# Bucketed attention and a two-layer network on one core: most first-batch heads loaded into both partition halves, operands made by factors per partition, score scale in the queries

## The chip, the cores and the metric

The kernel runs on one core of one Trainium2 chip. The metric is the device time of one execution in microseconds. Engines are named as in the profile: PE does matmuls and PEld loads their weights, DVE, ACT and POOL are the three elementwise engines, SP issues the DMAs. Three runs of the kernel before took 937.56, 939.98 and 940.53 us; the median, 939.98 us, is the time before.

## What is computed

Attention with a mask by hash buckets, and behind it a two-layer network with an exact gelu on the concatenated heads:

```python
batch, n_heads, seq, head_dim = (4, 8, 768, 64)      # q, k, v
q_bits = (np.einsum('bhsd,dk->bhsk', q, proj) > 0)   # proj: 64 x 6
k_bits = (np.einsum('bhsd,dk->bhsk', k, proj) > 0)
mask = q_bucket[:, :, :, None] == k_bucket[:, :, None, :]     # all six bits equal
scores = scale * np.matmul(q, k.transpose(0, 1, 3, 2))        # scale = 1 / sqrt(64)
scores = np.where(mask, scores, -1000000000.0)
attn = np.exp(scores - np.max(scores, axis=-1, keepdims=True))
attn = attn / (np.sum(attn, axis=-1, keepdims=True) + 1e-09)
out = np.matmul(attn, v)
...
h = x @ w_in                    # x: 3072 tokens x 512, w_in: 512 x 2048
g = 0.5 * h * (1.0 + erf(h * inv_sqrt2))
return (g @ w_out)              # w_out: 2048 x 512
```

## The kernel before

**Passes.** The four batches are walked in order. The first batch is done in two passes: pass 0 takes query columns 0 to 255 of all eight heads, pass 1 columns 256 to 767 of the eight heads in reverse order. The last three heads of pass 0 are made for all 768 queries and their operands are kept for pass 1 (`KEEP = 3`), so the first batch has 8 + 5 = 13 head loads. Batches 1 to 3 are one pass of eight heads each, 24 loads. A unit is 128 queries of one head against all 768 keys; there are 192, and 48 of them are in the first batch.

**A head** (`head`). Queries and keys of a head lie in one 128 x 768 tile: the queries transposed in partitions 0 to 63 (called the upper half here), the keys in 64 to 127 (the lower half). One DMA (L618) loads it into `rawe` (pass 0) or `raw` (later), rings of one buffer each. Then `high` (L621) rounds the tile to the fast matmul format into `Aq`. Three copies (`add_move`) put the rounded queries into the upper half of `Bq`, the rounded keys into the lower half of `Bk` and the rounded keys into the upper half of `Ak`; each may be on ACT, DVE, POOL (L377, L380) or a DMA (L625). Two subtractions raw minus rounded (`add_low`, L400, on DVE or POOL) give the low parts: of the queries into `Bq`'s lower half, of the keys into `Bk`'s upper half. Where operand sets share storage with the tiles of the later stage, the profile calls them `x` and `rest`.

**The hash.** Projections of both halves (L673, L675, L678) go to PSUM, their signs to `sign` (L681), and `mask_q` and `mask_k` write the signs as twelve extra rows into the lower halves of `Aq` and `Ak`, so that the score matmul adds a huge negative number for every bit that differs. The rest of those halves is zero (the clears at L338 and L434), or meets zeros.

**A unit** (`unit`). Scores come from two accumulating matmuls for each half of the keys (L716 on `Aq`, `Ak`; L717 on `Bq`, `Bk`). DVE takes the row maximum, negated (L720). `guard` (L724) makes the factor SCALE, or 0 where a row has no key in its bucket, and `shift` (L729) multiplies the maximum by it; both work on one column. ACT does the exp with this factor and shift (L732). In pass 0 and for three head pairs of pass 1 the whole probabilities are transposed by matmuls with a diagonal (L789), evicted to `pt` by ACT or DVE (L377, L380) and multiplied with the values in the slow format (L837). Elsewhere they are split in two halves (L748), transposed by DMA and multiplied by L846.

**The network.** Weights arrive as 64-bit words, are decoded on DVE (L466, L471, L476), scaled and split into high and low halves (`weight_pair`). The hidden layer is L1025, the gelu L1059, the output layer L1093.

**The order.** Nothing of the order is found at run time. `Plan.order` walks a model of the engines: each step has a key (a due time, from the numbers in `PAR`), a cost for each engine it may use, and the steps and buffers that it needs; the free engine takes the ready step with the lowest key. The steps of the network have late keys and are put wherever PE would be free. A step that may use several engines is placed by the first of them that is free and by the biases in `PAR` (such as `EV_ACT`). Each engine then executes its list in that order. DMAs all go through SP's list.

## Time and profile before

| | |
|---|---|
| median of three runs | 939.98 us |
| profiled execution, its own time | 939.12 us |
| its span | 937.3 us |
| mean granted PE clock | 0.987 |
| busy: PE, DVE, ACT, POOL | 883.2, 728.6, 612.7, 303.4 us |
| DMA | 122.81 MB in 300806 packets |

The span is the time from the first to the last instruction that the profiler recorded; the execution's own time is 1.8 us longer. Busy time is a share of the whole span, while the kernel has stages, so it is read by stretches of time. A matmul's record reaches into that of the next one, so mean durations of PE rows are longer than their distance.

### The profile page before, as it was taken

The page shows a single profiled execution, that of the slowest core. Times are in us where ns is not written, and L with a number is a line of the kernel's source. Part 1 is how long each engine was busy: PE and PEld are TensorE (multiplying, and loading weights), DVE is VectorE, ACT ScalarE, POOL GpSimd, SP SyncE. Part 2 cuts the span into 40 slices and gives each one's busy share as a digit, 9 for nine tenths or more (in the row PEclk, how much of TensorE's full clock was granted, in tenths as well). Part 3 has the DMA queues.
Part 4 walks back from the last instruction along what each step waited for, and adds up shares of the span by engine and source line. Part 5 has one row for each costly group of instructions (what it writes and reads, how often), then busy time and mean ns, then how long its engine had stood idle before and what let it go on. Part 6 is the DMA issues. An engine that isn't in the chain of part 4 may idle for free.

```text
span 937.3 us, 17819 instructions
## 1 busy us (share of the span) xinstructions
PE 883.2 (94%) x6728; PEld 642.8 (69%) x6728; DVE 728.6 (78%) x1616; ACT 612.7 (65%) x976; POOL 303.4 (32%) x254
## 2 busy tenths in 40 slices
PE   4777999887999999999999999999999999999998
PEld 3565788766676766677767776766777767676763
DVE  7899989899989899988889999989889971212122
ACT  5776877879776885867876777776788652222221
POOL 3652654556432233533142432342533100000000
PEclk9789999999999999999999999999999999999999
DMA  9456255277878699886787988687885850000000
GB/s 266 124 169 211 71 143 154 65 180 143 168 132 172 136 196 181 177 142 149 144 173 146 204 152 194 129 166 164 156 154 110 150 102 24 4 20 24 1 23 23
DMA packets 300806, 122.81 MB, mean 131 GB/s; under 512 B 241328, under 2 KB 285488, under 8 KB 300720
## 3 DMA queue, kind: packets, MB, share of 16 engines
q1 hardware_dynamic: 300544, 121.67, 59.5%
q8 instruction: 53, 0.87, 0.4%
q14 instruction: 33, 0.27, 0.1%
q10 hardware_dynamic: 176, 0.00, 0.0%
HBM read 45.49 MB, written 6.29 MB: 55 GB/s over the span
## 4 chain that ended last, share of the span: by engine, by line
PE 59%; DVE 7%; DMA 4%; ACT 3%; issue 1%; POOL 0%; ACTq 0%; SPq 0%; POOLq 0%; DVEq 0%
PE hp L1093 21%; PE hp L1025 21%; PE hp L846 6%; PE s L716 5%; PE s L717 4%; DVE hl L748 2%; DVE rows L720 2%; DMA vraw<-v 1%; DMA pt<-wraw 1%; DMA pt<-hl 1%; ACT p L732 1%; PE hp L673 1%; DVE wraw L748 1%; PE hp L678 1%; PE hp L675 1%
## 5 line engine op out<-in xcount | busy, mean ns | idle before, releaser
L1025 PE MATMUL hp<-x,Win 128*128 128x256 f16 x2304 | 267.9, 273 | 1.2 <-DVE rows L724 1.2
L1093 PE MATMUL hp<-Wout,g 128*128 128x512 f16 x1152 | 261.6, 379 | 0.0
L1025 PEld LDWEIGHTS <-Win 128*128 128x128 f16 x2304 | 220.3, 98 | 42.2 <-issue 13.5
L1093 PEld LDWEIGHTS <-g 128*128 128x128 f16 x1152 | 108.6, 98 | 128.4 <-issue 9.2
L720 DVE TENSOR_REDUCE rows<-s 128x1 f32<-128x768 f32 x192 | 179.5, 950 | 13.9 <-PE s L717 13.0
L732 ACT ACTIVATE p<-s,rows 128x768 f32<-128x768 f32 x143 | 141.3, 988 | 40.5 <-DVE rows L729 26.5
L716 PE MATMUL s<-Ak,Aq 128*128 128x384 f32 x352 | 137.8, 391 | 12.3 <-ACT p L732 6.0
L1035 ACT ACTIVATE h<-hp,ffs 128x512 f32<-128x512 f32 x96 | 65.8, 685 | 120.9 <-PE hp L1025 118.1
L717 PE MATMUL s<-Bk,Bq 128*128 128x384 f32 x352 | 120.5, 342 | 0.0
L380 DVE TENSOR_SCALAR g<-h,ffs 128x512 f16<-128x512 f32 x39 | 20.4, 526 | 112.4 <-ACT h L1059 81.7
L716 PEld LDWEIGHTS s<-Ak,Aq 128*128 128x128 f32 x352 | 67.6, 192 | 35.5 <-ACT p L732 12.4
L846 PE MATMUL hp<-pt,vhl 128*64 128x256 f16 x1368 | 82.3, 274 | 0.8 <-DMA pt<-hl 0.8
L846 PEld LDWEIGHTS <-vhl 128*64 128x64 f16 x1368 | 71.7, 110 | 12.7 <-issue 12.2
L1073 DVE SCALAR_TENSOR_TENSOR g<-h,ffs,g 128x512 f16<-128x512 f32 x96 | 77.0, 821 | 2.4
L748 DVE SCALAR_TENSOR_TENSOR hl<-p,rows,hl 128x768 f16<-128x768 f32 x72 | 76.2, 1061 | 2.1 <-ACT hl L377 1.0
L789 PE MATMUL hp<-dr,p 128*128 128x128 f32 x480 | 65.0, 290 | 6.3 <-DVE pt L380 2.4
L789 PEld LDWEIGHTS hp<-dr,p 128*128 128x128 f32 x480 | 61.1, 202 | 12.9 <-issue 3.3
L717 PEld LDWEIGHTS s<-Bk,Bq 128*128 128x128 f32 x352 | 68.0, 193 | 1.1
L732 ACT ACTIVATE wraw<-s,rows 128x768 f32<-128x768 f32 x49 | 48.4, 988 | 15.3 <-DVE hl L748 5.9
L681 ACT ACTIVATE sign<-hp,off 44x256 f32<-44x256 f32 (+1 forms) x74 | 41.6, 572 | 23.0 <-PE hp L678 21.0
L400 POOL TENSOR_TENSOR Bq<-raw,Aq 64x768 fp32r<-64x768 f32 (+1 forms) x23 | 40.9, 1779 | 22.6 <-ACT Aq L377 12.9
L380 POOL TENSOR_SCALAR hl<-p,rows 128x768 f16<-128x768 f32 x24 | 26.6, 1109 | 60.5 <-DMA pt<-hl 49.9
(154 smaller groups left out, 1258.9 us busy)
## 6 DMA issues: line engine op xcount, KB each, us to landing
raw<-qk SPq DMA_DIRECT2D x29, 384.0 KB, 3.6
vraw<-v SPq DMA_DIRECT2D x25, 384.0 KB, 4.1
wraw<-w_in SPq DMA_DIRECT2D x16, 512.0 KB, 4.3
wraw<-w_out SPq DMA_DIRECT2D x16, 512.0 KB, 5.1
out<-o SPq DMA_DIRECT2D x12, 512.0 KB, 2.8
Ak<-Aq SPq DMA_DIRECT2D x19, 192.0 KB, 3.3
rawe<-qk SPq DMA_DIRECT2D x8, 384.0 KB, 3.3
Bk<-Aq SPq DMA_DIRECT2D x16, 192.0 KB, 3.2
```

The source lines that it names most:

```text
L380: on.tensor_scalar(out=out, in0=in_, scalar1=scale, scalar2=bias, op0=ALU.mult, op1=ALU.add)
L716: nc.tensor.matmul(to, aq[:, qs], ak[:, n], start=True, stop=False)
L717: nc.tensor.matmul(to, bq[:, qs.start - q0 : qs.stop - q0], bk[:, n], start=False, stop=True)
L720: nc.vector.tensor_reduce(out=nm, in_=both(sp), axis=AX.XY, op=ALU.max, negate=True)
L732: nc.scalar.activation(out=buf(ex).rearrange("p (b k) -> p b k", b=2), in_=both(sp), func=AF.Exp, scale=sc, bias=nb, accum_out=ssum,)
L748: nc.vector.scalar_tensor_tensor(out=buf(hi)[:, 1], in0=buf(ex), scalar=r, in1=buf(hi)[:, 0], op0=ALU.mult, op1=ALU.subtract,)
L789: nc.tensor.matmul(buf(step[0])[:, (k - k0) * P : (k - k0 + 1) * P], buf(ex)[:, words(k)], buf(dg), start=True, stop=True,)
L846: nc.tensor.matmul(pv[j * D : (j + 1) * D], buf(vh)[:, tv, kt, j * D : (j + 1) * D], buf(holds[j][0])[:, tp * KT + kt, :nt], start=kt == 0 ...
L1025: nc.tensor.matmul(buf(pair[0])[:, j * ch[1] : (j + 1) * ch[1]], win_hl[:, f0 // WB1, tw, pr, f0 % WB1 : f0 % WB1 + P], x[:, tx, pr, : ch[1]],
L1035: nc.scalar.activation(out=bufs["h"][0][:, 2 * fp : 2 * fp + 2, :nt], in_=buf(pair[0])[:, : 2 * nt].rearrange("p (j k) -> p j k", j=2), fu ...
L1073: nc.vector.scalar_tensor_tensor(out=gt[:, 1, s2, :nt], in0=h[:, s2, :nt], scalar=sg, in1=gt[:, 0, s2, :nt], op0=ALU.mult, op1=ALU.subtract,)
L1093: nc.tensor.matmul(buf(banks[u]).rearrange("p (c f) -> p c f", c=NWB), gt[:, tg, f, u * P : (u + 1) * P], wout_hl[:, :, tw, ft], start=ft ...
```

## The change

`head` gets an argument `twice`, true for the first batch except for the first two heads of pass 0 (`OLD = 2`): eleven head loads. For these:

- The keys are loaded twice, into both halves of a raw buffer, and the queries twice, into both halves of another one; only the columns that are needed. These are four DMAs in place of one. `raw` and `rawe` get two buffers each.
- No copies are made. A factor per partition does the work of the halves: `Ak` is the loaded keys times (1, 0), rounded; `Bk` is the loaded keys times (-1, 1) plus `Ak`, so minus the low part above and the keys themselves below; `Aq` is the queries times SCALE, rounded; `Bq` is the queries times (0, SCALE) minus `Aq`. The two roundings may be on ACT, DVE or POOL, the two others are `scalar_tensor_tensor` on DVE.
- The projection takes one matmul more for each stretch of columns in which queries are projected, since high queries and high keys are in separate tiles; its constants are `hash_lo`, `hash_neg` and `hash_both`.
- The early operand sets hold only 256 queries in `Aq` too, and `Ak` is cleared for the first two sets only.

For the 26 other heads the rounding has a factor per partition (SCALE for queries, 1 for keys), and the low part of the queries is a `scalar_tensor_tensor` on DVE only. For all units the score scale is thus in the queries, and `guard` and `shift` become one instruction over two columns. `sign` is bf16. All numbers of `PAR` are others, and it has four new ones (`QL`, `QH0` to `QH2`).

```diff
-RAWE = 1
+RAWE = 2
+RAWS = 2
+OLD = 2
...
-        "s": 2, "hp": 4, "p": 2, "hl": 2, "raw": 1, "rawe": RAWE, "sign": 1, "dr": 2, "pt": NTH + 1,
+        "s": 2, "hp": 4, "p": 2, "hl": 2, "raw": RAWS, "rawe": RAWE, "sign": 1, "dr": 2, "pt": NTH + 1,
...
-        "sign": ring(const, "sign", [2 * 32, S], F32, 1),
+        "sign": ring(const, "sign", [2 * 32, S], BF16, 1),
...
-            early.tile([P, q_first if nm == "Bq" else S], F32R, tag=f"{nm}{i}", name=f"{nm}{i}")
+            early.tile([P, q_first if nm[1] == "q" else S], F32R, tag=f"{nm}{i}", name=f"{nm}{i}")
...
+    nc.gpsimd.memset(rows[:, :, 0], 1.0)
+    only_up, only_low, minus_up, fold = factors = [
+        const.tile([P, 1], F32, tag=f"half{i}", name=f"half{i}") for i in range(4)
+    ]
+    for t, (up, down) in zip(factors, ((1.0, 0.0), (0.0, SCALE), (-1.0, 1.0), (SCALE, 1.0))):
+        nc.gpsimd.memset(t[:D], up)
+        nc.gpsimd.memset(t[D:], down)
...
+    nc.vector.tensor_scalar(
+        out=hash_neg[:, both_bits], in0=hash_hi[:, both_bits].bitcast(F32), scalar1=minus_up, scalar2=None,
+        op0=ALU.mult,
+    )
...
-    for n, (_, ak, _, _) in enumerate(sets[1:]):
+    for n, (_, ak, _, _) in enumerate(sets[:OLD]):
...
+        if twice:
+            def add_load(half, cols, more):
+                box = []
+                def load():
+                    n = cols.stop - cols.start
+                    for to in range(2):
+                        nc.sync.dma_start(
+                            out=buf(box[0])[to * D : (to + 1) * D, :n], in_=qk[b, h, half * D : (half + 1) * D, cols]
+                        )
+                n = cols.stop - cols.start
+                box.append(
+                    add("SP", 0.02 + 1.84e-3 * n, load, key - PAR["HQ"] + more, takes="rawe" if first else "raw")
+                )
+                return box[0]
+            rk = add_load(1, slice(0, S), 0)
+            rq = add_load(0, qr, PAR["QL"])
+            def key_high():
+                affine(hk.engine, ak, buf(rk), only_up)
+            def key_low():
+                nc.vector.scalar_tensor_tensor(
+                    out=bk, in0=buf(rk), scalar=minus_up, in1=ak.bitcast(F32), op0=ALU.mult, op1=ALU.add
+                )
+            def query_high():
+                affine(hq.engine, aq[:, qb], buf(rq)[:, :nq], SCALE)
+            def query_low():
+                nc.vector.scalar_tensor_tensor(
+                    out=bq[:, qb], in0=buf(rq)[:, :nq], scalar=only_low, in1=aq[:, qb].bitcast(F32),
+                    op0=ALU.mult, op1=ALU.subtract,
+                )
+            hk = add(affine_on("RND", S, True), 0, key_high, key, [rk, *clear], port=True)
+            lk = add("DVE", subtract_cost("DVE", S), key_low, key + PAR[f"LOW{cl}"], [hk], port=True)
+            hq = add(affine_on("RND", nq), 0, query_high, key + PAR[f"QH{cl}"], [rq, *clear], port=True)
+            lq = add("DVE", subtract_cost("DVE", nq), query_low, key + PAR[f"DUP{cl}"], [hq], port=True)
+            free(rk, [lk])
+            free(rq, [lq])
...
-            affine(hi.engine, aq, buf(raw))
+                affine(hi.engine, aq, buf(raw), fold)
...
-        lq = add_low(nq, bq[D:, qb], top, qr)
+            def query_low():
+                nc.vector.scalar_tensor_tensor(
+                    out=bq[D:, qb], in0=buf(raw)[:D, qr], scalar=SCALE, in1=aq[:D, qr].bitcast(F32),
+                    op0=ALU.mult, op1=ALU.subtract,
+                )
...
-                nc.tensor.matmul(pp, hash_lo, aq[:, n], start=True, stop=False)
+                if twice and with_q:
+                    nc.tensor.matmul(pp, hash_lo[:, KR:], aq[:, at], start=True, stop=False)
+                if twice:
+                    nc.tensor.matmul(pp, hash_lo[:, :HR], ak[:, n], start=not with_q, stop=False)
+                else:
+                    nc.tensor.matmul(pp, hash_both, aq[:, n], start=True, stop=False)
...
-            nc.vector.tensor_scalar(
-                out=sc, in0=nm, scalar1=BIG / 2, scalar2=SCALE, op0=ALU.is_lt, op1=ALU.mult
-            )
-        def shift():
-            nc.vector.tensor_scalar(out=nb, in0=nm, scalar1=sc, scalar2=None, op0=ALU.mult)
+            nc.vector.scalar_tensor_tensor(
+                out=st[:, 2:4], in0=nm.broadcast_to([P, 2]), scalar=BIG / 2, in1=st[:, :2],
+                op0=ALU.is_lt, op1=ALU.mult,
+            )
...
+                twice = b == 0 and (n_pass > 0 or pos >= OLD)
```

More of the change, by code (lines that the diff above doesn't have):

```diff
@@ L280, in tile_bucket_attention_moe @@
     ]
[L281 removed]
+    rows = const.tile([P, NT, 7], F32, tag="rows", name="rows")
     tiny = const.tile([P, 4 * NSC + 2 * B, 4], F32, tag="tiny", name="tiny")
@@ L606, in values_halves, with head @@
         return hi, lo
-    def head(b, h, i, key, clear, qr, cl):
+    def head(b, h, i, key, clear, qr, cl, twice):
         aq, ak, bq, bk = sets[i]
@@ L640, in add_low @@
-        def add_low(n, out, rows, cols):
-            box = []
-            box.append(
-                add(
-                    subtract_on("LO", n), 0,
-                    lambda: subtract(box[0].engine, out, buf(raw)[rows, cols], aq[rows, cols].bitcast(F32)),
-                    key + PAR[f"LOW{cl}"], [hi], port=True,
-                )
-            )
-            return box[0]
-        top, end = slice(0, D), slice(D, P)
-        raw = add("SP", 1.43, load, key - PAR["HQ"], takes="rawe" if first else "raw")
@@ L665, in head @@
+        space = add("none", 0, lambda: None, key, [lq, lk], takes="sign")
         signs = []
@@ L684, in sign @@
                 )
-            box.append(add("PE", 0.04 + (0.46e-3 * (2 + with_q)) * (c1 - c0), project, key + PAR[f"PRJ{cl}"], [space], takes="hp"))
+            box.append(add("PE", 0.04 + (0.46e-3 * (2 + (1 + twice) * with_q)) * (c1 - c0), project, key + PAR[f"PRJ{cl}"], [space], takes="hp"))
             signs.append(add("ACT", affine_cost("ACT", c1 - c0, True) + 0.09, sign, key + PAR[f"PRJ{cl}"], box))
@@ L695, in mask_k, with unit @@
             affine(r2.engine, ak[D : D + 2 * NBIT], rows, BIG / 2, -BIG / 2)
-        r1 = add(affine_on("MSK", nq), 0, mask_q, key + PAR[f"MSK{cl}"], [*signs, m2, m3], port=True)
+        r1 = add(affine_on("MSK", nq), 0, mask_q, key + PAR[f"MSK{cl}"], [*signs, *masked], port=True)
         r2 = add(affine_on("MSK", S), 0, mask_k, key + PAR[f"MSK{cl}"], signs, port=True)
         free(space, [r1, r2])
-        return [m3, r1, r2]
-    def unit(t, i, q0, qs, cl, whole, made, place):
+        return [*masked[1:], r1, r2]
+    def unit(t, i, q0, qa, qs, cl, whole, made, place):
         aq, ak, bq, bk = sets[i]
         st = rows[:, t % NT]
-        nm, sc, nb, ssum, si, r = (st[:, k : k + 1] for k in range(6))
+        nm, sc, nb, ssum, si, r = (st[:, k : k + 1] for k in range(1, 7))
         def both(step):
@@ L763, in unit @@
         mx = add("DVE", 0.87, top, t - PAR[f"MX{cl}"], [sp])
-        sh = add("DVE", 0.07, guard, t - PAR[f"EX{cl}"], [mx])
-        sh = add("DVE", 0.07, shift, t - PAR[f"EX{cl}"], [sh])
+        sh = add("DVE", 0.1, guard, t - PAR[f"EX{cl}"], [mx])
         ex = add("ACT", 0.98 + 0.23 * (si_on == "ACT"), exps, t - PAR[f"EX{cl}"], [sh], takes="p", table="exp")
@@ L938, in tile_bucket_attention_moe @@
                 cols = (0, S) if more and pos >= len(heads) - KEEP else (q0, q1)
-                made = head(b, h, i, t - lead, last_use.get(i, cleared.get(i, [])), cols, cl)
-                owner[i] = (b, h, cols[0], made)
-            _, _, base, made = owner[i]
+                twice = b == 0 and (n_pass > 0 or pos >= OLD)
+                made = head(b, h, i, t - lead, last_use.get(i, cleared.get(i, [])), cols, cl, twice)
+                owner[i] = (b, h, cols[0], cols[0] if twice else 0, made)
+            _, _, base, abase, made = owner[i]
             used[i] = n_pass * len(heads) + pos
@@ L947, in tile_bucket_attention_moe @@
                     qs = slice(ch[0] + u * P, ch[0] + (u + 1) * P)
-                    sp, tr = unit(t, i, base, qs, cl, whole, made, (holds[h % 2, ch], u))
+                    sp, tr = unit(t, i, base, abase, qs, cl, whole, made, (holds[h % 2, ch], u))
                     uses.append(sp)
```

102 lines of the change are left out of this document (60 added, 42 removed).

## Prediction

> **What bounds the kernel now.** First the page's slices, because the busy shares average over stages with different limits.
>
> ```profile
> PE 883.2 (94%) x6728; PEld 642.8 (69%) x6728; DVE 728.6 (78%) x1616; ACT 612.7 (65%) x976; POOL 303.4 (32%) x254
> ...
> PE   4777999887999999999999999999999999999998
> ...
> DVE  7899989899989899988889999989889971212122
> ...
> PEclk9789999999999999999999999999999999999999
> ```
>
> The reader is to see two stages. Until about the eleventh slice (250 us) PE has gaps and DVE has almost none; behind it PE is full to the end, and after 780 us DVE is nearly idle: only the hidden layers are left there. The windows put numbers on it (columns: length; busy PE, PEld, DVE, ACT, POOL; clock; DMA share; GB/s).
>
> ```profile
> 0.00:100.00 100.00, 68.72 (x437) 53.89 (x437) 88.25 (x194) 65.58 (x124) 47.21 (x46) 0.91 0.62 186
> 100.00:250.00 150.00, 138.21 (x1115) 110.40 (x1115) 137.89 (x323) 121.75 (x221) 82.38 (x64) 0.98 0.53 130
> 250.00:780.00 530.00, 523.36 (x4144) 377.36 (x4144) 468.13 (x1047) 385.48 (x587) 173.83 (x145) 1.00 0.78 156
> 780.00:938.00 158.00, 152.91 (x1038) 101.20 (x1035) 34.29 (x55) 39.90 (x45) 0.00 (x0) 1.00 0.04 14
> ```
>
> Before 250 us DVE is busy 226.1 of 250 us, ACT 187.3, POOL 129.6, and PE stands idle for 31.3 + 11.8 = 43.1 us. PE work that could fill that time exists (the hidden layers fill in wherever they may), so each microsecond by which the first batch and the weights are ready sooner takes one from the end, as long as PE stays full afterwards. From 250 to 780 us PE shows only 6.6 us idle. The first batch of heads, which the change is about, is made in the DVE-bound stage.
>
> Then the waits of SP's queue from 0 to 100 us, and two rows of the timeline:
>
> ```profile
> SPq L618 <- POOL Bk L400: 16.7, 4, 6.7
> ```
>
> ```profile
> 23.45 2.14 POOL L400 TENSOR_TENSOR x<-rawe,x 64x768 fp32r<-64x768 f32 x1
> ...
> 23.93 1.93 DVE L400 TENSOR_TENSOR rest<-rawe,x 64x256 fp32r<-64x256 f32 x1
> ```
>
> The load of the next head (L618) stands in SP's order until POOL has taken the low part of the last head's keys, for 16.7 us in four waits, and what SP would issue behind it (weights, values, transposes) waits too. And a DVE subtraction of 64x256 that overlaps a POOL subtraction ends 0.27 us after it and takes 1.93 us.
>
> **The change, part by part.** Eleven of the thirteen head loads of the first batch change (pass 0: three with 256 queries, three with all 768; pass 1: five with 512). The rows of 0 to 250 us, in which all of them lie:
>
> ```profile
> L400 POOL TENSOR_TENSOR Bk<-raw,Aq 64x768 fp32r<-64x768 f32 x5 | 10.0, 2005 | 0.4
> L400 POOL TENSOR_TENSOR Bk<-rawe,Aq 64x768 fp32r<-64x768 f32 x4 | 8.1, 2024 | 0.3
> L400 POOL TENSOR_TENSOR x<-raw,x 64x768 fp32r<-64x768 f32 x2 | 4.1, 2053 | 0.1
> L400 POOL TENSOR_TENSOR Bq<-raw,Aq 64x512 fp32r<-64x512 f32 x3 | 4.1, 1375 | 0.2
> L400 POOL TENSOR_TENSOR x<-rawe,x 64x768 fp32r<-64x768 f32 x2 | 4.0, 1990 | 0.1
> ...
> L400 POOL TENSOR_TENSOR rest<-rawe,x 64x768 fp32r<-64x768 f32 x1 | 2.1, 2140 | 0.1
> ...
> L400 POOL TENSOR_TENSOR Bq<-rawe,Aq 64x256 fp32r<-64x256 f32 x2 | 2.0, 980 | 0.1
> ...
> L400 POOL TENSOR_TENSOR Bq<-rawe,Aq 64x768 fp32r<-64x768 f32 x1 | 1.8, 1807 | 0.1
> L380 POOL TENSOR_SCALAR Bk<-Aq 64x768 fp32r<-64x768 f32 x6 | 6.9, 1158 | 16.3 <-ACT Aq L377 16.2
> L377 ACT ACTIVATE Ak<-Aq 64x768 fp32r<-64x768 f32 x8 | 6.8, 844 | 0.2
> L400 DVE TENSOR_TENSOR rest<-raw,x 64x512 fp32r<-64x512 f32 x2 | 1.4, 685 | 0.1
> L400 DVE TENSOR_TENSOR Bq<-rawe,Aq 64x768 fp32r<-64x768 f32 x1 | 1.0, 952 | 0.4 <-ACT Aq L377 0.4
> L400 DVE TENSOR_TENSOR Bq<-rawe,Aq 64x256 fp32r<-64x256 f32 x2 | 0.8, 419 | 1.8 <-ACT Aq L377 1.8
> L729 DVE TENSOR_SCALAR rows<-rows 128x1 f32<-128x1 f32 x55 | 10.5, 208 | 0.4
> L724 DVE TENSOR_SCALAR rows<-rows 128x1 f32<-128x1 f32 x55 | 7.5, 149 | 0.3
> L380 DVE TENSOR_SCALAR pt<-hp 128x384 f32<-128x384 f32 x53 | 28.6, 550 | 3.6 <-PE hp L789 2.8
> ```
>
> *Low parts go to DVE alone.* All eleven key subtractions and seven of the query subtractions of these heads ran on POOL, 11 x 2.0 + (2.0 + 2.1 + 1.8 + 4.1) = 32 us by the POOL rows (two of the five `Bk<-raw` belong to batch 1). DVE had the other four queries, 4.3 us: 1.93, 0.95 and 1.4. The new ones are DVE scalar_tensor_tensor over 128 partitions; a duration here follows the columns, not the partitions. Priced by the DVE rows (419, 685, 952 ns; 1.05 us for 768 allowing a little contention): keys 11 x 1.05 = 11.6, queries 3 x 0.42 + 5 x 0.69 + 3 x 1.0 = 7.7. DVE: +19.3 - 4.3 = **+15.0**. Upper price: the same 64x768 subtraction beside POOL's in batches 1 to 3 below, 1608 against 952 ns, so up to 0.66 us more for each of the 22: +14.5.
>
> *Moves go.* Three copies for each head, 33 in all: 13 on ACT (12 x 0.84 + 0.42 = 10.5 us), 9 on POOL (some 9.4 us at 0.6 to 1.3 each), 11 by DMA. What is added for them: a pass over the queries, 3 x 0.42 + 5 x 0.63 + 3 x 0.84 = 6.9 us, which any of three engines may take (0.63 interpolated between 0.42 and 0.84). So POOL loses about 41 us of work, ACT 10.5, and they get about 7.
>
> *Score scale in the queries.* L724 and L729 (149 + 208 ns) become one scalar_tensor_tensor over two columns, which must cost between the two and perhaps a little more: 0.18 us. Before 250 us: 55 x (0.357 - 0.18) = **-9.6 us** of DVE. In the pass over the rows the start of the exp moves up by one hop.
>
> *Relief of DVE by the freed engines.* The placing is free among ACT, DVE and POOL for the evictions of `pt` (ACT or DVE), for the scaling and splitting of weights, and for diagonals. DVE holds 28.6 us of the first. Lower bound 0 (all stays). Upper bound 25 us, evictions handed over until DVE and ACT carry the same: DVE 226.1 + 15.0 - 9.6 - 3 (contention, below) = 228.5, ACT 187.3 - 10.5 + 3 = 180, half the difference. I take **-10**, nearer the lower end, because ACT's slices show 7 to 8 tenths already where PE needs the evictions at once.
>
> *Contention.* The 18 two-input POOL instructions that go mean fewer DVE instructions that are held up:
>
> ```profile
> L466 DVE TENSOR_SCALAR Win<-wraw 128x512 int32<-128x512 int32 x16 | 11.8, 740 | 0.7 <-DMA wraw<-w_in 0.5
> L466 DVE TENSOR_SCALAR Wout<-wraw 128x512 int32<-128x512 int32 x16 | 6.7, 425 | 1.3 <-DMA wraw<-w_out 1.2
> L400 DVE TENSOR_TENSOR Bq<-raw,Aq 64x768 fp32r<-64x768 f32 x4 | 6.4, 1608 | 0.1
> L400 POOL TENSOR_TENSOR Bq<-raw,Aq 64x768 fp32r<-64x768 f32 x20 | 36.8, 1839 | 22.4 <-ACT Aq L377 12.9 <-DVE Aq L380 6.5 <-PE s L717 2.0
> ```
>
> The same decoding of weights costs 740 ns early, 425 later: 5 us. I take **-3** (bounds 0 and -5).
>
> *Loads.* The timeline's issues, the first landing, and the page's time to landing of a copy:
>
> ```profile
> 22.15 0.48 SPq L625 DMA_DIRECT2D rest<-x  x1
> ...
> 25.93 0.34 SPq L618 DMA_DIRECT2D rawe<-qk  x1
> ```
>
> ```profile
> 5.58 0.84 ACT L377 ACTIVATE Aq<-rawe 128x768 fp32r<-128x768 f32 x1 [1.85 <-DMA rawe<-qk]
> ```
>
> ```profile
> Ak<-Aq SPq DMA_DIRECT2D x19, 192.0 KB, 3.3
> ```
>
> One DMA becomes four, keys twice and queries twice: 33 more issues, 11 moves fewer, so 22 more on SP at 0.34 to 0.48 us, some 9 us in 250 us, behind which transposes and weights queue; and since a head's keys and queries take both buffers, the next key load waits in SP's order for DVE's low part of the keys. Bytes grow by 3 x 128 + 3 x 384 + 5 x 256 KB = 2.8 MB and fall by some 2 MB of moves; the DMA share of 0.53 to 0.62 hides that. Against it stands the 16.7 us wait of L618 that ends: the buffers are two, and a short DVE step frees them. The chain to the first projection loses its copy (a DMA copy takes 3.3 us to land) and gets nothing. Bounds -6 and +4; I take **-2**.
>
> *PE.* One projection matmul more wherever queries are projected: starts in the timeline are 0.11 us apart for 256 columns and 0.23 for 512:
>
> ```profile
> 49.27 0.27 PE L675 MATMUL hp<-Bq,hash_hi 128*44 128x256 f32 x1
> 49.39 0.28 PE L678 MATMUL hp<-Bk,hash_hi 128*44 128x256 f32 x1
> 49.50 0.39 PE L673 MATMUL hp<-Aq,hash_lo 128*44 128x512 f32 x1
> 49.73 0.40 PE L678 MATMUL hp<-Bk,hash_hi 128*44 128x512 f32 x1
> ```
>
> 3 x 0.11 + 3 x 0.34 + 5 x 0.23 = 2.5 us, mostly in PE's 43 us of gaps: **+1**. The few constants at the start and the per-partition factor in the rounding I cost at nothing: they lie before the first load lands at 5.58 us, or are below 0.1 us each on engines with room.
>
> *Batches 1 to 3.* The heads stay as they were but for the query's low part, now on DVE alone: 24 x 1.0 us against the 6.4 us row, +17.6; guard and shift -137 x 0.177 = -24.2; POOL is free of the 36.8 us row. DVE is 6.6 us better off, and PE can only give back its 6.6 us there: **-1.5** (bounds 0 and -6.6).
>
> Sum: DVE before 250 us +15.0 - 9.6 - 10 - 3 = -7.6; loads -2; PE +1; later -1.5: -10.1 us. The profiled execution took 939.12 us (span 937.3); 929.0, which against the median of 939.98 us is **930 us**.
>
> **A rule against it.** Trainium skill, SBUF — State Buffer, section "Who interferes with whom": a VectorE instruction with two SBUF inputs contends with a GpSimd instruction that reads SBUF, and which is issued first decides who waits. The pair at 23.45 and 23.93 us agrees. By it the 22 new low parts collide with whatever POOL is given; that is the second rival below, priced there from rows, and the sum by it is that rival's 950 us.
>
> **Rivals.** *Hidden anyway.* The freed engines take nothing from DVE, whose balance is then +15.0 - 9.6 - 3 = +2.4, and the loads' -2 and the later -1.5 cancel it: 939 to 940 us. For it: placing is by due times set by hand, not by load. Against it: DVE's evictions have ACT as an alternative, and ACT has 62 us free before 250. Chance 0.12.
>
> *DVE becomes longer (slower).* The low parts are paid at the contended price: +15.0 - 9.6 + 14.5 - 10 = +9.9, PE +1: 950 us. It decides as soon as contention exceeds what leaves DVE, about 0.35 us for each low part (7.6 / 22). For it: the rows of 1608 and 1933 ns. Against it: POOL's long partner instructions are the ones that disappear, and a plain POOL pass is 0.8 to 1.3 us. Chance 0.18.
>
> *More than I sum.* If DVE is relieved to the bound (+15.0 - 9.6 - 25 - 3 = -22.6), loads give 6 and the later stage its 6.6: 939.1 - 22.6 - 6 - 6.6 + 1 = 905 us. That end is unlikely, half of the way to it (917) is not; it is within the forecast's chance.
>
> **How the numbers follow.** Forecast, faster: 0.70, its own range 917 to 937. About 0.3% (2.8 us) is what a measurement of this kernel can tell from no change. Same 0.12, slower 0.18. For 8 in 10, the low end is 914 (a little beyond 917), the upper end lies between no change and the slow rival's 950: 945.
>
> **What would show it.** Right: POOL subtractions before 250 us down by about 18, the copies of Ak and Bk there down from 16 heads to five, the first hidden-layer matmul and the last exp of the first batch some 5 to 10 us sooner; the wait of L618 on POOL gone; evictions moved from DVE to ACT. Wrong: DVE low parts at 1.3 us and more for 768 columns, PE gaps before 250 us still at 43 us or more, SP's queue waiting on loads, or new PE gaps after 250 us from DVE being behind with the transposed halves.

## Result and the profile after

The changed kernel takes **963.24 us** (median; 960.2 to 967.2), the kernel before beside it 940.25 us: ratio **1.025** (95% interval 1.0224 to 1.0275), 23 us slower. The forecast was 930 us. The profiled execution took 963.43 us, its span 961.6 us, at a mean granted PE clock of 0.979 (before 0.987).

The page's first two parts, in the form that the prediction shows of before:

```profile
PE 892.5 (93%) x6742; PEld 644.1 (67%) x6742; DVE 732.3 (76%) x1435; ACT 610.5 (63%) x981; POOL 266.5 (28%) x237
...
PE   4778899976999899999999999999999999999998
...
DVE  6889998997889789998898899999997762222122
...
PEclk9789899997999999999999999999999999999999
```

The stretches by windows (columns as in the prediction: length; busy PE, PEld, DVE, ACT, POOL; clock; DMA share; GB/s):

```profile
0.00:100.00 100.00, 69.47 (x452) 55.15 (x453) 84.00 (x180) 64.06 (x124) 32.39 (x46) 0.90 0.69 194
100.00:250.00 150.00, 133.20 (x1060) 104.14 (x1059) 133.49 (x262) 112.79 (x212) 64.40 (x53) 0.95 0.49 125
250.00:780.00 530.00, 512.73 (x3993) 368.25 (x3991) 469.98 (x922) 385.61 (x591) 169.75 (x138) 1.00 0.78 154
780.00:962.00 182.00, 177.08 (x1244) 116.52 (x1242) 44.81 (x72) 48.07 (x57) 0.00 (x0) 0.99 0.09 24
```

DVE is 8.6 us less busy before 250 us than it was (84.00 + 133.49 against 226.1) and POOL 32.8 us less, but PE's idle time there is 47.3 us instead of 43.1, and from 250 to 780 us it is 17.3 instead of 6.6. At 780 us, 24.2 us more PE work is left (177.08 against 152.91). Of these, 14.9 us are gaps in PE, 10.7 of them behind 250 us, where before there were nearly none. The other 9.3 us are a PE that is busy for longer (892.5 us against 883.2 in the whole run). Two things go with that: 14 more matmuls of the projections, which the prediction prices at 2.5 us, and a lower granted clock, 0.95 against 0.98 from 100 to 250 us. What each of them adds was not measured apart.

What ended PE's gaps from 250 to 780 us is in the view of its waits, of after and then of before (us in total, times, longest; L813 and L732 are the exps):

```profile
PE s L799 <- ACT wraw L813: 4.4, 6, 1.4
PE s L799 <- ACT p L813: 4.3, 9, 1.4
PE hp L761 <- DMA Bk<-Aq: 4.2, 3, 2.0
```

```profile
PE s L716 <- ACT p L732: 3.2, 7, 0.9
...
PE s L716 <- ACT wraw L732: 0.7, 2, 0.5
```

So PE waits 4.8 us longer for exps there (8.7 against 3.9), and 4.2 us for a DMA for which it did not wait before.

The first hidden-layer matmul comes later too, by the timelines of before and of after:

```profile
112.56 0.61 PE L1025 MATMUL hp<-x,Win 128*128 128x256 f16 x4
```

```profile
121.42 1.48 PE L1106 MATMUL hp<-x,Win 128*128 128x256 f16 x12
```

**The merged guard.** The groups of after between 0 and 250 us give the merged `guard` (L807) and the low parts:

```profile
L402 DVE TENSOR_SCALAR pt<-hp 128x384 f32<-128x384 f32 x36 | 19.0, 547 | 1.5 <-PE hp L869 1.0 <-PE hp L437 0.2
L807 DVE SCALAR_TENSOR_TENSOR rows<-rows 128x2 f32<-128x2 f32 x53 | 18.4, 355 | 0.2
L668 DVE SCALAR_TENSOR_TENSOR Bk<-rawe,half,Ak 128x768 fp32r<-128x768 f32 x4 | 4.1, 1013 | 0.0
L668 DVE SCALAR_TENSOR_TENSOR Bk<-raw,half,Ak 128x768 fp32r<-128x768 f32 x3 | 3.0, 1005 | 0.0
L676 DVE SCALAR_TENSOR_TENSOR Bq<-raw,half,Aq 128x512 fp32r<-128x512 f32 x3 | 2.2, 742 | 0.0
...
L732 DVE SCALAR_TENSOR_TENSOR Bq<-rawe,Aq 64x256 fp32r<-64x256 f32 x2 | 1.9, 942 | 0.0
```

and the view of one line (minimum/median/maximum in ns) shows it in the whole run, with its group behind it; then, of before, `shift`, which it replaces, and the exps that waited for that (us, times):

```profile
L807 DVE SCALAR_TENSOR_TENSOR rows<-rows x192: 141/154/2000, 16.1 to 777.4; 128x2 f32<-128x2 f32 x192
```

```profile
L807 DVE SCALAR_TENSOR_TENSOR rows<-rows 128x2 f32<-128x2 f32 x192 | 59.9, 318 | 1.3
```

```profile
L729 DVE TENSOR_SCALAR rows<-rows x192: 194/209/221, 14.3 to 757.6; 128x1 f32<-128x1 f32 x192
...
  ACT p L732: 26.5, 26
```

The median, 0.154 us, is below the 0.18 us forecast. But some of the 192 take up to 2.0 us, while `shift` with its one input never took more than 0.221. One of the held ones, with what POOL does at that time:

```profile
239.59 2.13 POOL L422 TENSOR_TENSOR Wout<-o,Wout 128x1024 f16<-128x1024 f32 x1 [1.85 <-ACT Wout L399]
```

```profile
241.01 0.72 DVE L807 SCALAR_TENSOR_TENSOR rows<-rows 128x2 f32<-128x2 f32 x1
```

POOL's subtraction ends at 241.72, the guard at 241.73. The guard now has two inputs from SBUF (`nm` and the pair of factors), and an instruction of two elements in each partition waits for the end of POOL's 1024. By the trace, 40 of the 192 guards take over 0.25 us; each of the 40 overlaps a POOL instruction that began before it, and ends with it. About half of these are POOL passes with one input, as here, where POOL ends at 323.06 and the guard at 323.07:

```profile
322.15 0.91 POOL L402 TENSOR_SCALAR wraw<-p,rows 128x768 f16<-128x768 f32 x1 [2.02 <-DVE Bq L732]
```

```profile
322.42 0.65 DVE L807 SCALAR_TENSOR_TENSOR rows<-rows 128x2 f32<-128x2 f32 x1
```

The exp stands behind the guard, and PE behind the exp. The exps' own wait for the guard does not show the loss: it is 16.9 + 5.2 us (tiles `p` and `wraw`), less than the 26.5 + 5.7 us for `shift` before. PE's waits for the exps do: 14.8 + 4.8 us in the whole run, against 7.1 + 0.7.

**The start.** The first rounding has a factor per partition, and the load of ACT's table now stands in front of it only when the raw tile has landed. ACT's timeline of before, then of after:

```profile
2.44 1.28 ACT L377 ACT_TABLE_LOAD   x1 [2.44 <-issue]
5.58 0.84 ACT L377 ACTIVATE Aq<-rawe 128x768 fp32r<-128x768 f32 x1 [1.85 <-DMA rawe<-qk]
```

```profile
5.38 1.28 ACT L399 ACT_TABLE_LOAD   x1 [5.38 <-DMA rawe<-qk]
6.68 0.93 ACT L399 ACTIVATE Aq<-rawe,half 128x768 fp32r<-128x768 f32 x1
```

**Queues.** SP's waits from 0 to 100 us, of after and then of before:

```profile
SPq L481 <- DVE Win L498: 20.9, 9, 3.7
SPq L649 <- DVE Bq L676: 7.4, 3, 4.0
```

```profile
SPq L459 <- DVE Win L476: 17.2, 12, 3.1
```

The 16.7 us wait for POOL's low part is gone. SP's longest wait, for the decoding of weights, was there before and is 3.7 us longer now; the loads wait 7.4 us for a low part of queries on DVE. The wait of L761 among PE's waits above is a projection (the hash) of the heads that are not loaded twice, for the DMA that copies their keys. In the plan of before the hash step needs `[m1, m2, lq, lk]`, where `m1` and `m2` are two of the copies; the change left `[lq, lk]`. The planner no longer knows that the projection stands behind these copies and can put it too early.

### The profile page after: what moved, and what is told of

It is laid out like the page before. It is cut to its first block, busy times and chain, and to the rows that moved or that the text cites. A ratio compares the mean times of both kernels' runs of the same rounds, so it can differ in the third digit from the quotient of the medians.

```text
span 961.6 us, 17646 instructions
## 1 busy us (share of the span) xinstructions
PE 892.5 (93%) x6742; PEld 644.1 (67%) x6742; DVE 732.3 (76%) x1435; ACT 610.5 (63%) x981; POOL 266.5 (28%) x237
## 4 chain that ended last, share of the span: by engine, by line
PE 44%; DVE 5%; DMA 4%; ACT 2%; issue 1%; POOL 0%; ACTq 0%; POOLq 0%; DVEq 0%
PE hp L1174 18%; PE hp L1106 15%; PE hp L926 4%; PE s L799 3%; PE s L800 2%; DMA pt<-hl 2%; DVE rows L803 1%; DVE hl L829 1%; DMA pt<-wraw 1%; DVE rows L807 1%; DVE wraw L829 1%; ACT p L813 1%; DMA Bk<-Aq 0%; ACT wraw L813 0%; PE hp L758 0%
## 5 line engine op out<-in xcount | busy, mean ns | idle before, releaser
L813 ACT ACTIVATE p<-s,rows 128x768 f32<-128x768 f32 x140 | 138.2, 987 | 56.2 <-DVE rows L807 16.9
L926 PEld LDWEIGHTS <-vhl 128*64 128x64 f16 x1368 | 71.6, 110 | 13.3 <-issue 13.1
L1154 DVE SCALAR_TENSOR_TENSOR g<-h,ffs,g 128x512 f16<-128x512 f32 x96 | 75.0, 795 | 7.2 <-POOL g L402 4.3
L829 DVE SCALAR_TENSOR_TENSOR hl<-p,rows,hl 128x768 f16<-128x768 f32 x65 | 68.7, 1060 | 3.3 <-ACT hl L399 1.6
L813 ACT ACTIVATE wraw<-s,rows 128x768 f32<-128x768 f32 x52 | 51.3, 987 | 18.7 <-DVE hl L829 8.5
L807 DVE SCALAR_TENSOR_TENSOR rows<-rows 128x2 f32<-128x2 f32 x192 | 59.9, 318 | 1.3
L422 POOL TENSOR_TENSOR Bk<-raw,Aq 64x768 fp32r<-64x768 f32 x23 | 44.7, 1942 | 43.3 <-ACT Aq L399 38.4
L764 ACT ACTIVATE sign<-hp,off 44x256 bf16<-44x256 f32 (+1 forms) x74 | 41.4, 569 | 14.1 <-PE hp L761 12.9
```

What stands on the lines that cost most here:

```text
L807: nc.vector.scalar_tensor_tensor(out=st[:, 2:4], in0=nm.broadcast_to([P, 2]), scalar=BIG / 2, in1=st[:, :2], op0=ALU.is_lt, op1=ALU.mult,)
L813: nc.scalar.activation(out=buf(ex).rearrange("p (b k) -> p b k", b=2), in_=both(sp), func=AF.Exp, scale=sc, bias=nb, accum_out=ssum,)
L829: nc.vector.scalar_tensor_tensor(out=buf(hi)[:, 1], in0=buf(ex), scalar=r, in1=buf(hi)[:, 0], op0=ALU.mult, op1=ALU.subtract,)
L926: nc.tensor.matmul(pv[j * D : (j + 1) * D], buf(vh)[:, tv, kt, j * D : (j + 1) * D], buf(holds[j][0])[:, tp * KT + kt, :nt], start=kt == 0 ...
L1154: nc.vector.scalar_tensor_tensor(out=gt[:, 1, s2, :nt], in0=h[:, s2, :nt], scalar=sg, in1=gt[:, 0, s2, :nt], op0=ALU.mult, op1=ALU.subtract,)
```

## Experiments

Each has its verdict against the kernel before on the same chip. "Searched" means that the numbers of `PAR` were searched at random by the finishing time that the kernel's own planner gives for its order, which changes the order of the work and the placing among the engines, and no work. All results first, with PE's idle time in the profiled execution (780 us less the busy PE of the windows to 780 us):

| run | work | order | us | ratio, 95% interval | PE idle, 0-250 + 250-780 |
|---|---|---|---|---|---|
| before | | its own | 939.98 | | 43.1 + 6.6 |
| changed | | its own | 963.24 | 1.0224 to 1.0275 | 47.3 + 17.3 |
| a_two | changed, two guards | as changed | 953.26 | 1.0111 to 1.0185 | 41.5 + 13.8 |
| b_stt | before, `shift` with two inputs | as before | 957.27 | 1.0151 to 1.0211 | 48.6 + 12.2 |
| a_par | changed | PAR of before | 975.26 | 1.0344 to 1.0414 | 52.4 + 22.2 |
| a_par_two | changed, two guards | PAR of before | 975.83 | 1.0351 to 1.0414 | 53.6 + 20.2 |
| b_jit | before | the same list | 939.26 | 0.9986 to 1.0012 | 43.4 + 6.9 |
| b_lq | before, query low on DVE | PAR of before | 955.19 | 1.0143 to 1.0198 | 50.0 + 7.0 |
| d_twice | double loads alone | PAR of before | 961.99 | 1.0209 to 1.0262 | 46.8 + 11.9 |
| c_par_two | all but double loads, two guards | PAR of before | 981.96 | 1.0429 to 1.0479 | 49.6 + 27.5 |
| o_before | before | searched | 942.16 | 0.9987 to 1.0025 | 47.0 + 3.0 |
| o_twice | double loads alone | searched | 940.17 | 0.9964 to 1.0016 | 40.8 + 10.7 |
| o_best | the same, truer prices | searched | 943.99 | 1.0040 to 1.0074 | 41.7 + 7.6 |
| o_tlq | double loads, other query low on DVE | searched | 941.10 | 1.0001 to 1.0053 | 43.9 + 9.6 |
| o_lq | before, query low on DVE | searched | 952.31 | 1.0120 to 1.0180 | 49.5 + 8.9 |
| o_scale | all but double loads, two guards | searched | 943.39 | 1.0009 to 1.0063 | 45.3 + 7.6 |
| o_all | changed, two guards | searched | 949.88 | 1.0063 to 1.0117 | 43.1 + 13.1 |
| o_all2 | the same | searched from elsewhere | 944.20 | 1.0035 to 1.0098 | 42.9 + 7.6 |
| o_stt | changed, merged guard | searched | 948.40 | 1.0060 to 1.0107 | 45.0 + 10.9 |
| o_port | the same, guard marked | searched | 943.54 | 0.9992 to 1.0048 | 44.6 + 5.7 |

### The guard in a fixed order: a_two, b_stt

```diff
 a_two, on the changed kernel, in its order
-nc.vector.scalar_tensor_tensor(out=st[:, 2:4], in0=nm.broadcast_to([P, 2]), scalar=BIG / 2, in1=st[:, :2], ...)
+nc.vector.tensor_scalar(out=nb, in0=nm, scalar1=BIG / 2, scalar2=nm, op0=ALU.is_lt, op1=ALU.mult)
+nc.vector.tensor_scalar(out=sc, in0=nm, scalar1=BIG / 2, scalar2=1.0, op0=ALU.is_lt, op1=ALU.mult)
 b_stt, on the kernel before, in its order
-nc.vector.tensor_scalar(out=nb, in0=nm, scalar1=sc, scalar2=None, op0=ALU.mult)
+nc.vector.scalar_tensor_tensor(out=nb, in0=nm, scalar=1.0, in1=sc, op0=ALU.mult, op1=ALU.mult)
```

> The changed kernel in the same order on every engine, but the one guard instruction with two inputs in SBUF is issued as two tensor_scalar instructions with one input each. Theory GUARD (the new guard is held up by POOL: median 154 ns, but mean 318 and up to 2000 ns, 192 of them, and the exps wait): its 31 us of DVE time above the median go and the time falls from 963 to 940-952 us. Theory ORDER (the new due times give a worse order): the order is unchanged, so 958-966 us. Theory LOADS (double loads, and low parts on DVE alone, cost the time): 958-966 us.

> The kernel before in the same order on every engine; only shift is issued as a scalar_tensor_tensor with two inputs in SBUF in place of a tensor_scalar with a pointer. Nothing else of the change is in it. Theory GUARD: shift's mean goes from 209 ns to about 350-450 and the time from 940 to 950-965 us. Theories ORDER and LOADS: 938-944 us.

Two instructions in place of one are 10.0 us faster (963.24 to 953.26), 1.3 us short of what theory GUARD expected. And the kernel before, with nothing changed but the form of `shift`, is some 17 us slower, inside that theory's range. In both pairs every engine has the same list of instructions but for the guard or `shift`. By line, a_two's guards (L807, L810) and b_stt's `shift` (L729), and who waited for it:

```profile
L807 DVE TENSOR_SCALAR rows<-rows x192: 193/205/216, 16.8 to 766.5; 128x1 f32<-128x1 f32 x192
```

```profile
L810 DVE TENSOR_SCALAR rows<-rows x192: 135/144/147, 17.0 to 766.6; 128x1 f32<-128x1 f32 x192
```

```profile
L729 DVE SCALAR_TENSOR_TENSOR rows<-rows x192: 139/159/2024, 14.1 to 775.2; 128x1 f32<-128x1 f32 x192
...
  ACT p L734: 40.0, 35
```

With one input from SBUF none of 384 is held; with two, on one column, the longest is 2.024 us and the exps wait 40.0 us for it (26.5 us for the old form). In a_two PE's gaps are 9.3 us shorter than in the changed kernel (41.5 + 13.8 against 47.3 + 17.3), and its waits for exps are 11.6 + 2.7 us against 14.8 + 4.8. This is the form of the instruction, and nothing else of the change. The Trainium skill, SBUF — State Buffer, section "Who interferes with whom", has this rule: a VectorE instruction with two SBUF inputs contends with a GpSimd one that reads SBUF, and order of issue, not shape, decides who blocks. The traces agree, down to one column (159 ns at the median, 2024 held).

### The parts in an order that was not made for them: a_par, a_par_two, b_lq, d_twice, c_par_two, b_jit

```diff
 a_par, a_par_two: PAR of before in the changed kernel, with the merged guard and with two
 b_lq, on the kernel before
-subtract_on("LO", n), 0,
+({"DVE": (subtract_cost("DVE", n), 0.0)} if rows.start == 0 else subtract_on("LO", n)), 0,
 d_twice: the changed kernel's double loads, with scale, query low part, guard, shift and PAR of before
 c_par_two, on the changed kernel with two guards, PAR of before and one buffer each for raw and rawe
-twice = b == 0 and (n_pass > 0 or pos >= OLD)
+twice = False
 b_jit, on the kernel before: each number of PAR moved by up to 2
```

> The changed kernel with the due times of the kernel before (the four new ones kept). Theory ORDER: 940-952 us. Theories GUARD and LOADS: 960 us or more, since the old due times were made for other costs.

> Both: the due times of the kernel before and the guard as two single-input instructions. Theory GUARD alone: as the run with the two instructions, within some 8 us. Theory ORDER alone: as the run with the old due times. If both add up: 930-940 us. Theory LOADS: 955 us or more in all four runs but the second.

> The kernel before with the low part of the queries allowed on DVE only (it was on POOL for 27 of 37 heads); the order is planned anew with the old due times. Theory LOADS in its part 'low parts on DVE alone': 948-956 us, the 12 us that are left when the guard is issued as two instructions. Theory ORDER: as the control with moved due times. Otherwise 940-945 us.

> The double loads of eleven heads alone, two buffers each, on the kernel before, with guard, shift, scale, the other 26 heads and the due times as before. Theory that the double loads cost the time: 950-976 us (the changed kernel with the old due times took 975). Theory that they gain what I forecast for the first batch: 930-938 us. If the old due times do not fit the new steps: over 960 us, and the run with the new ones has to tell.

> The changed kernel without double loads (no head is loaded twice, one raw buffer each), with the guard as two single-input instructions and the old due times: what stays is the score scale in the queries by a factor per partition and the low part of the queries on DVE. Theory that the double loads cost the time: 938-945 us. Theory that the DVE-only low part does: as the run that has it alone, 948-956 us.

> Control: the kernel before with each due time and bias of PAR moved by a random amount between -2 and 2; same instructions, another order. It measures what a new order costs by itself. Theory ORDER (the order is balanced finely, any new one costs): 945-960 us. Theories GUARD and LOADS: within 0.5% of 940 us.

In d_twice one projection stands ahead of the copy of keys that it reads, because the plan's needs were those of the change. Its signs come from what the buffer held, so this run's result is not the function above; the amount of work is the same.

With the numbers of before the query low parts cost 16 us, the double loads 22 and the rest of the change without them 42, and the whole change 34 to 35 instead of 23. And the guard, worth 10 us in the changed kernel's order, is worth nothing here (975.26 and 975.83): PE has some 74 us of gaps with either form. Old due times in the changed kernel were to give 940 to 952 us if only the new ones were at fault, and gave 975; the 982 us of c_par_two are above all that was expected. So these runs do not price the parts. They price them in an order that was not made for them and, b_lq apart, in a plan that also lacks the two needs of the hash step. b_jit was to be the control for that and is none: its list of instructions is the same on every engine, so it repeats the kernel before.

### The same parts in searched orders: o_before, o_twice, o_scale, o_all

`o_before` had its PAR scrambled first and is the control. The three others are the work of d_twice, c_par_two and a_two. In them the hash step has its needs again, and in o_scale and o_all the step with the two guards is priced 0.14 us instead of 0.1:

```diff
-space = add("none", 0, lambda: None, key, [lq, lk], takes="sign")
+space = add("none", 0, lambda: None, key, [lq, lk] if twice else [m1, m2, lq, lk], takes="sign")
```

> The kernel before with every part as it is and only the order made anew: all numbers of PAR were moved at random (spread 25) and then searched again by the finishing time that the kernel's own planner gives for its order. It is the control for the three runs beside it, whose orders were searched in the same way. Theory O (the parts cost what their durations say, and most of what is lost beyond the guard is lost by orders that the planner thinks good and the chip does not): another order of the same work costs 5 to 20 us by itself, 945 to 960 us. Theory W (the work itself is dearer, whatever the order): 937 to 943 us.

> The kernel before with the double loads of the first batch's heads alone (factors per partition in their high and low parts; the scale stays in the exponential, guard and shift stay two instructions, the other heads' query low parts may run on POOL), with the plan's needs complete and PAR searched anew. With the numbers of before the same part took 962.0 us. Theory O: 930 to 942 us, as the copies and the POOL subtractions of 26 heads are gone. Theory W: 950 to 962 us.

> The changed kernel without the double loads: all heads are loaded once and copied as before, the scale is in the high parts by a factor per partition, the query low parts of all 48 heads run on DVE, guard and shift are two instructions with one input, the plan's needs are complete and PAR is searched anew. With the numbers of before the same part took 982.0 us. Theory O: 938 to 950 us. Theory W: 965 us or more. If this one stays above the double loads alone by 8 us or more under either theory, the query low parts on DVE are a cost of their own.

> The changed kernel with three edits: guard and shift as two instructions with one input each, the plan's hash step of the other heads waiting for their copies again (the change dropped these two from what the step needs), and PAR searched anew by the planner's own finishing time. The run with the two guards alone took 953.3 us. Theory O: what is left of the loss is order, 935 to 945 us. Theory W: the low parts with a factor per partition, the query low parts on DVE and the second load stay, 950 to 956 us.

The control is at 942.2 us: this other, searched order of the same work costs nothing that can be told. Against it the expectation of 945 us or more from theory O fails. The parts, however, fall by 22 us (d_twice 962.0 to o_twice 940.2) and 39 us (c_par_two 982.0 to o_scale 943.4). Neither was dear work. And neither gains. Needs and order were changed together here, so the fall is not divided between them. The changed kernel's work with two guards comes down by 3.4 us only, to 949.9, between what the two theories expected. The dependency's wait, by PE's waits in o_all, falls to 0.2 us (4.2 in the changed kernel):

```profile
PE hp L761 <- DMA Bk<-Aq: 0.2, 1, 0.2
```

### Where the rest of o_all is: o_lq, o_tlq, o_all2, o_best

```diff
 o_lq: b_lq, searched
 o_tlq, on o_twice
-lq = add_low(nq, bq[D:, qb], top, qr)
+lq = add_low(nq, bq[D:, qb], top, qr, True)     # True: DVE only
 o_all2: o_all, its PAR scrambled (spread 25), searched again
 o_best, on o_twice: prices of the plan, searched again
-sh = add("DVE", 0.07, guard, t - PAR[f"EX{cl}"], [mx])
+sh = add("DVE", 0.14, guard, t - PAR[f"EX{cl}"], [mx])
...   (shift likewise; low parts with a factor 0.07 dearer)
```

> The kernel before with the query low parts of all 48 heads on DVE alone and PAR searched anew; with the numbers of before this took 955.2 us. The two-input guard is not in it. Theory Q (query low parts on DVE are what keeps the changed kernel with two guards and a searched order at 949.9 us): 945 us or more. Theory O (only the order was wrong): 938 to 944 us.

> The double loads alone (scale in the exponential, two guards), but with the query low parts of the other 26 heads on DVE alone, PAR searched anew. The double loads alone with these subtractions free to go to POOL took 940.2 us, all edits together 949.9 us. Theory Q: 946 to 952 us. Theory S (the scale, by a factor per partition in the high parts, and the multiplying low parts make the 9 us): 938 to 943 us.

> The same work as the changed kernel with two guards and complete needs (949.9 us with one searched order), with another order: PAR moved at random (spread 25) and searched anew from there. Theory W (the work of this combination is dearer): 947 to 953 us again. Theory O (it is a matter of which order the search ends in): anywhere between 938 and 955 us, off the first by over 3 us.

> The double loads alone again (940.2 us), with the planner told what the trace measured: low parts with a factor 0.07 us dearer, guard and shift 0.14 us each instead of 0.07; PAR searched anew. Theory O: an order made with truer prices is better, 928 to 938 us, below the kernel before. Theory W: the double loads are worth nothing at any order, 938 to 943 us.

Against the kernel before, the query low parts on DVE cost 13 us in one setting (o_lq, 952.3, as theory Q expected) and 2 to 3 where other parts of the change stand beside them (o_tlq 941.1, o_scale 943.4), so they have no price of their own either. In o_lq they were held more than in o_tlq:

```profile
L400 DVE TENSOR_TENSOR Bq<-raw,Aq 64x768 fp32r<-64x768 f32 x24 | 33.8, 1407 | 0.7
```

```profile
L422 DVE TENSOR_TENSOR Bq<-raw,Aq 64x768 fp32r<-64x768 f32 x24 | 25.6, 1067 | 0.7
```

That does not account for the 13 us alone: in b_lq the same row has a mean of 1093 ns, and the kernel is 16 us slower.

o_all2 is the same work as o_all in another order and takes 5.7 us less by the medians. Each beside the kernel before on its own chip, the ratios are 1.0090 and 1.0066, and their intervals overlap. So it points to the order and is no proof by itself. Truer prices in the plan (o_best) did not make the double loads gain: 944.0 us is above what either theory expected.

### The merged guard in a searched order: o_stt, o_port

```diff
 o_stt: changed kernel, needs complete, guard priced 0.16, searched
 o_port, on that
-sh = add("DVE", 0.16, guard, t - PAR[f"EX{cl}"], [mx])
+sh = add("DVE", 0.16, guard, t - PAR[f"EX{cl}"], [mx], port=True)
```

A step marked `port=True` is not started by the planner while POOL works, and the other way round; the low parts carry this mark, the guard did not.

> The changed kernel with its merged guard kept as it is (one instruction, two inputs from SBUF, priced 0.16 us in the plan), the plan's needs complete, PAR searched anew. It stands beside the two searched orders with two guards (949.9 and 944.2 us). Theory G (the merged guard is held by POOL's two-input instructions whatever the order): the guard's mean stays at 0.30 us or more with the longest at 2 us, and the time is 8 us or more above those two, 953 to 962 us. Theory O (the guard's loss belongs to one order): 944 to 950 us.

> As the run beside it, and the guard's step is marked port=True, as the low parts are: the planner then puts no guard beside a POOL step. Theory G: the marked low parts were never held in the changed kernel (1004 to 1020 ns), so the marked guard isn't either: mean 0.15 to 0.20 us, none or few near 2 us. What DVE wins is partly paid by POOL and DVE standing aside for one another: 940 to 952 us. Against it: if the guard is still held (mean 0.30 us or more), the mark doesn't do it, and the low parts were spared by chance.

The group of the guard in o_stt, then in o_port:

```profile
L807 DVE SCALAR_TENSOR_TENSOR rows<-rows 128x2 f32<-128x2 f32 x192 | 60.2, 322 | 1.5
```

```profile
L807 DVE SCALAR_TENSOR_TENSOR rows<-rows 128x2 f32<-128x2 f32 x192 | 38.1, 212 | 0.9
```

In a new order the guard is held as before (322 ns; 318 in the changed kernel). But the time is 948.4, between the two searched orders with two guards and 14.8 us below the changed kernel, which has the same guard. So the guard being held is a property of the instruction; what it costs (10, 17, 0, and here nothing that can be told) depends on the order around it. With the mark it takes 212 ns instead of 322, longer than the 0.15 to 0.20 expected, since the longest still takes 2.04 us. This version keeps all of the change and takes 943.5 us (ratio 1.002, 0.9992 to 1.0048), which can't be told from the kernel before. No version that was run is faster than the kernel before by more than the noise. The exps of o_port wait 47.1 + 13.3 us for the guard, longer than the 16.9 + 5.2 in the changed kernel, which is 20 us slower: the sum of a wait is not its cost.

o_port also tests what the forecast rested on. Its windows:

```profile
0.00:100.00 100.00, 66.97 (x395) 51.29 (x397) 79.62 (x168) 60.17 (x109) 37.67 (x49) 0.90 0.71 195
100.00:250.00 150.00, 138.47 (x1124) 111.07 (x1121) 125.78 (x270) 119.12 (x234) 67.53 (x60) 0.97 0.49 123
250.00:780.00 530.00, 524.30 (x4107) 377.88 (x4107) 471.33 (x936) 400.96 (x606) 148.81 (x132) 1.00 0.75 151
```

DVE is busy 205.4 us before 250 us, 20.7 less than in the kernel before, and PE's gaps there are 44.6 us, not fewer than 43.1. (By then 54 row maxima are done instead of 56, so a little of the 20.7 us is work not yet done.) And the windows of o_twice and of o_before:

```profile
0.00:100.00 100.00, 68.71 (x442) 53.94 (x443) 81.09 (x187) 57.72 (x117) 33.86 (x49) 0.91 0.68 194
100.00:250.00 150.00, 140.47 (x1143) 112.47 (x1142) 134.86 (x316) 126.74 (x232) 67.50 (x52) 0.97 0.54 133
250.00:780.00 530.00, 519.32 (x4104) 374.34 (x4103) 458.52 (x1041) 388.45 (x594) 194.46 (x158) 1.00 0.80 156
```

```profile
0.00:100.00 100.00, 68.83 (x425) 55.90 (x427) 80.81 (x178) 65.50 (x124) 50.12 (x50) 0.88 0.56 166
100.00:250.00 150.00, 134.13 (x1072) 105.92 (x1072) 137.23 (x312) 120.76 (x225) 73.59 (x61) 0.94 0.56 137
250.00:780.00 530.00, 527.00 (x4178) 382.13 (x4177) 473.85 (x1063) 396.22 (x604) 151.56 (x128) 1.00 0.80 158
```

The double loads in a searched order do what was forecast in direction: 2.3 us fewer gaps before 250 us. Behind it there are 4.1 us more. The scrambled and searched kernel before does the opposite, 3.9 more and 3.6 fewer. In the seven searched runs that are at 944.2 us or less the two gaps add up to 49.3 to 53.5 us (49.7 before), so none has less of them by more than 0.4 us. Besides, PE is busy for longer in all seven, 883.8 to 888.3 us against 883.2. That need not be more work: o_before, with the work unchanged, has 886.6 us at a mean granted clock of 0.978 (0.987 before).

## Why the prediction was wrong

**The step that failed first is the guard's price.** "0.18 us" was taken between two rows of one-input instructions, for an instruction with two inputs from SBUF. Before 250 us it was to save 9.6 us and later 24.2. Measured: 18.4 us against 7.5 + 10.5 before, so nothing before 250 us; later 59.9 - 18.4 = 41.5 us, against 46.6 before (27.0 + 37.6 in the whole run, less 18.0). The rule that would have told it stood in the prediction, applied to the 22 low parts and not to the 192 guards. It also lies between the maximum and the exp, on every unit's chain. That is 10 of the 23 us, shown with the order held fixed, and it is the price in that order only.

**The step that failed most deeply is the first one**: that DVE's busy time before 250 us sets the end there, so that each microsecond off it comes off the end. In the changed kernel DVE fell by 8.6 us, nearly the forecast -7.6, and PE's gaps there grew from 43.1 to 47.3 us. That agreement is luck: the four terms as measured (low parts +14.9, guard +0.4, evictions -9.6, decoding -3.3) add up to +2.4, and the rest is at least in part work not done by then, 53 guards instead of 55. The first hidden matmul came 8.9 us later, by itself a weak sign, since o_before has it at 139.3 us and takes 942.2. In o_port DVE fell by 20.7 us and PE's gaps didn't. Over the seven searched runs at 944.2 us or less DVE is busy 205.4 to 220.8 us before 250 us, in all of them less than the 226.1 before, and PE's gaps are 40.8 to 47.0 us without following it: 44.6 for the least DVE time, 45.3 for the most. A DVE at 9 tenths in the slices was read as the bound, and in these orders it wasn't. What does set PE's 41 to 47 us of gaps there, the runs do not show.

**A term that was missing: the order.** All PAR numbers are new, and the prediction let the order carry over at no cost. The same work with two guards was run in four orders: 944.2, 949.9, 953.3 and 975.8 us, the last two without the two needs. That spread is larger than any term of the sum. Part of it in the changed kernel is the dropped need of the hash step: the wait for `Bk<-Aq` is 4.2 us of the 10.7 us of new gaps behind 250 us, and 0.2 in o_all, where the need is back. How many microseconds of the end this is was not measured apart from the order. Of the 13 us that remain with two guards, 3 to 9 went with needs and order (o_all, o_all2); the last 4 us of o_all2 (0.35 to 0.98%) are not gaps (50.5 us to 780 us, 49.7 before) but a PE busy for 887.1 us instead of 883.2. Why it is busy for longer stays open.

**Too small a term: PE.** The sum has +1 us for PE. PE is busy for 9.3 us longer, as said with the result.

**Right, term by term.** *Low parts:* with those of the kept heads the keys take 11.1 us (forecast 11.6) and the queries 8.1 (7.7), none held: 1.0 us for 768 columns; the upper price of +14.5 was not paid. These steps are marked in the plan as steps that keep clear of POOL; whether that is why they were spared was not tested on them. *Relief:* evictions on DVE 28.6 to 19.0 us, -9.6 for a forecast of -10. *Contention:* the first decoding step of the weights fell from 18.5 us to these rows' 15.2, -3.3 for -3 (the held guards are counted above):

```profile
L488 DVE TENSOR_SCALAR Wout<-wraw 128x512 int32<-128x512 int32 x16 | 8.4, 540 | 2.6 <-DMA wraw<-w_out 2.5
L488 DVE TENSOR_SCALAR Win<-wraw 128x512 int32<-128x512 int32 x16 | 6.8, 422 | 4.9 <-DMA wraw<-w_in 4.9
```

*Loads:* the wait for POOL went, as said. *POOL's subtractions* of first-batch heads are gone: of the heads' it has two before 250 us, and these are batch 1's:

```profile
L422 POOL TENSOR_TENSOR Bk<-raw,Aq 64x768 fp32r<-64x768 f32 x2 | 3.6, 1817 | 0.2
```

**Costed at nothing, and not nothing:** the factor per partition in the first rounding, 1.1 us later at the start because its table load lost its cover (5.58 to 6.68). *Batches 1 to 3* were to give 1.5 us and lost 10.7 in PE's gaps. New gaps there were among the named signs of being wrong, but from transposed halves that come late; for those PE waited 0.2 us.

**The rivals.** "DVE becomes longer" named the right mechanism, two-input instructions held by POOL, at the wrong instruction, and its 950 us is near the 953.3 that remains *without* the guard, which is chance. "Hidden anyway" (939 to 940) has the number that the double loads alone reach once their order is searched (940.2, and 944.0 with other prices), but not the mechanism: the evictions did leave DVE (-9.6), and that did not help.

## What to carry to other kernels

Before two small instructions are merged into one, count the inputs that come from SBUF: here the merge that added the second one let POOL hold any of its executions for up to 2.0 us, on the chain to the exp. Where a hand-made or searched order carries a kernel, a part taken alone in the old order measures the misfit with that order too, so search the order again for each variant, with a scrambled and searched control. And an engine at 90% is not the bound until a run with less of its work is faster.

## What the hardware showed that was not expected

- A DVE instruction of one column with two inputs from SBUF takes 0.159 us at the median and up to 2.024 us beside POOL; the same work with one input is never over 0.221 us. POOL passes with one input hold it as well as POOL's subtractions do, 0.65 us in the pair at 322 us above.
- A factor per partition in the first activation moves the load of ACT's table (1.28 us) behind the arrival of that activation's data: issued at 5.38 us instead of 2.44. The other runs agree: 5.14 us in o_scale, which has the factor and no double loads; 2.43 in o_twice, which has the double loads and a first rounding without the factor. It lengthens the rounding itself from 0.84 to 0.93 us; the Trainium skill, ScalarE: Activation LUTs, section "What ACT_TABLE_LOAD costs", has 93 ns for such an operand, and the rows agree.
- A planner's mark doesn't keep two engines apart with certainty: the two query low parts over 64x256 carry it and took 0.942 us each in the changed kernel and 1.980 in o_port, both times while a POOL instruction ran, where the kernel before has 0.419 for that width. The row is o_port's:

```profile
L732 DVE SCALAR_TENSOR_TENSOR Bq<-rawe,Aq 64x256 fp32r<-64x256 f32 x2 | 3.9, 1980 | 0.0
```
